# One fused attention and expert kernel: a head's bucket bits from four 32-column tiles, and new orders of TensorE and of the copies

## The chip, the cores and the metric

The kernel runs on one core of one Trainium2 chip. The metric is device time in microseconds (us). Beside it there is one profiled execution, whose trace names every instruction with its start and duration. Engines are named as in the profile: PE is TensorE's matrix multiply, PEld its weight load, DVE VectorE, ACT ScalarE, POOL GpSimd, SP the engine that issues nearly all transfers. TensorE's granted clock is 1.00 of its upper level (2.4 GHz) in every stretch of the execution before.

## The reference, cut to what matters

Sixteen heads (2 batches of 8) of 768 tokens and 64 features. Six projections give each query and key six sign bits; a query sees only the keys with the same six bits.

```
q_bits = (einsum('bhsd,dk->bhsk', q, proj) > 0)          # proj is 64 x 6
k_bits = (einsum('bhsd,dk->bhsk', k, proj) > 0)
mask   = q_bucket[..., :, None] == k_bucket[..., None, :]  # bucket = sum of bits * 2**j
scores = where(mask, scale * q @ k.T, -1e9)
attn   = softmax(scores)
x      = (attn @ v) as 1536 tokens x 512 features
x      = max(x @ w1, x @ w2, x @ w3) @ w_out             # 768 hidden features
out    = g(x @ w_in) @ w_out2                            # 2048 hidden features, g piecewise
```

## The kernel before, in words

Attention fills roughly the first 207 us, the two expert layers the rest. The first expert matmuls stand behind the last attention matmul on PE.

Of attention the work is cut into 96 tiles of 128 queries against all 768 keys, six tiles to a head. A tile goes through: the score block `t_qk` on PE (four matmuls into one of two `s_ps` buffers; the mask is part of the matmul, since rows 64 to 75 of `qb` and `hi` hold scaled bits); `t_max` on DVE; `t_exp` on ACT; then either six transposes `t_tr` on PE into `t_ps` and a copy `t_out` on ACT or DVE (head 0 and the odd heads), or `t_turn` on DVE ("turned" heads: 2, 4, and so on to 14). Three transposed tiles make a group, and `g_pv` multiplies it by the values on PE into `u_ps` in two pieces: first 2 matmuls, then 4. A turned head is multiplied by `block4`: 96 matmuls on tiles of 32 rows by 64 columns that run side by side. `g_copy` and `copy4` on ACT empty the results, and SP folds and moves them.

Bits of head h are made ahead of its first tile. `bits_both` puts two matmuls of 64 columns and 384 tokens into `pj_ps` (the two halves of the head, one in partitions 0 to 63, one in 64 to 127). Two comparisons `bits_rows` on DVE write 44 rows by 384 tokens each into rows 64 to 107 of `qb`: the query's bits stand where they are used, and the key's bits in rows 96 to 107 are moved by one transfer, `prep_move(h, "kb")`, into rows 64 to 75 of `hi`. Then the head's first score block may start.

The order of everything is made when the program is built. PE's order is written by hand as strings: `q5` is the score block of the tile in slot 5, `t` its transposes, `b` the bits that go with a group, `v` and `w` the first and second piece of a group's (or turned head's) value matmuls, `r` the transposition of row sums, `m` an early piece of the first expert layer. `first_part` stands first, `period` five times, `last_part` last. For the other engines a planner (`Work`) walks through tasks with an assumed cost, an assumed `lag` after it (for a transfer: until it has landed) and a due time shifted by `SHIFT`, and writes instructions in the order in which it would start them. The hardware then runs each engine's list in that order.

Of the kernel before, what the change touches and what calls it, by code (L numbers as in the profile page):

```python
# [22 lines left out]
HALF = S // 2  # L23
MASKED = 1.0e9
# [89 lines left out]
def lsh_attention_moe_kernel(  # L114
# [29 lines left out]
    pj_raw = const.tile([128, 64], F32, name="pj_raw")  # L144
# [137 lines left out]
    def attention(mlp_steps):  # L282
        with ExitStack() as ax, ExitStack() as sx:
# [54 lines left out]
            def pj_sign():  # L338
                rows = pj_raw.rearrange("p (a b) -> p a b", a=2)[:, :, 0:6]
                nc.gpsimd.tensor_scalar(out=rows, in0=rows, scalar1=-1.0, scalar2=0.0, op0=ALU.mult, op1=ALU.add)  # L340
# [58 lines left out]
            def bits_mm(h, half, bank, first):  # L399
                nc.tensor.matmul(  # L400
                    out=bank[first:first + 64, 0:HALF], lhsT=pj_raw if h else pj_sc,
# [98 lines left out]
            ahead = s_ps[1][:, 0]  # L500
# [111 lines left out]
            nc.gpsimd.tensor_tensor(out=pj_sc, in0=pj_raw, in1=pj_by, op=ALU.mult)  # L612
# [20 lines left out]
            T_AT, P_AT = 2, 1  # L633
            START = {h: min(SLOT[NK * h + t] for t in range(NK)) for h in range(NH)}
# [4 lines left out]
            SHIFT = {t_exp: 42.5, t_out: 2.0, g_copy: 17.5, copy4: -82.0, pair_copy: -20.5, w_tick: 60.0, bits_rows: 4.5, t_max: -12.5, t_turn: 8.0, pair_recip: 20.0}  # L639
# [8 lines left out]
            scaled, moves, r_place, order = {}, {}, {}, {}  # L648
            raw_s["prep"].free.pop()
            raw_s["r"].free.pop()  # L650

            def head_tasks(h):
# [14 lines left out]
                q = task("SP", 0.6, due, prep_both, h, after=[hi], lag=4)  # L667
                ql = task("SP", 0.5, due + 1, prep_move, h, "ql", after=lo, lag=3.5)
                kh = task("SP", 0.5, due + 2, prep_move, h, "kh", after=[ql], lag=3.5)
                scaled[h], moves[h], r_place[h] = hi, [q, ql, kh], rp  # L670
                if h == 1:
                    bp = place("b", 1)
                    mm = task("PE", 0.644, due + 1, bits_both, h, after=[hi], takes=[bp], leaves=[rp])
                    order["bits"] = [mm]
                    rows = [
                        task("DVE", 0.69, due + 1, bits_rows, h, half, pj_ps, 64 * half, after=[mm]) for half in range(2)
                    ]
                    rows[1]["leaves"] = [bp]
                    bits_task(h, rows, due + 1)
# [431 lines left out]
```

## Time and profile before

| what | before |
|---|---|
| median of 3 runs | 668.01 us (667.34 to 668.87) |
| the profiled execution's own time | 667.27 us |
| its span in the profile | 665.5 us |
| PE busy over the span | 658.9 us (99%) |
| DVE, ACT, POOL busy | 488.2, 340.6, 275.5 us |
| last attention matmul to first expert block on PE | at 207.3 us |

The span is what the profile's instructions cover; the execution's own time holds 1.77 us more. PE's busy time counts a matmul from its start to the end of its own pipeline, so that neighbours overlap: what a block costs is read from its start to the start of the next block.

### The profile page before, as it was taken

To read this page: it belongs to the slowest core of one execution; us is meant where nothing else is said; L and a number is where in the kernel's file an instruction comes from. 1 tells how busy PE (TensorE), PEld (TensorE's weight loads), DVE (VectorE), ACT (ScalarE), POOL (GpSimd) and SP (SyncE) were. 2 spreads that over 40 slices of the span, in tenths; PEclk is the share of its full clock that TensorE was granted. 3 is DMA by queue.
4 is the path that set the end of the run, shared out by engine and by line. 5 is a ranking of instruction groups with operands and counts; after the bars stand their busy time and mean duration, and the time that the engine had idled before them with its cause. 6 is when DMAs were issued, how large, how long until landed. Compare 5 with 4: busy or idle time off the path is not lost.

```text
span 665.5 us, 11771 instructions
## 1 busy us (share of the span) xinstructions
PE 658.9 (99%) x4541; PEld 528.6 (79%) x4541; DVE 488.2 (73%) x718; ACT 340.6 (51%) x631; POOL 275.5 (41%) x252
## 2 busy tenths in 40 slices
PE   8999999999999999999999999999999999999998
PEld 6668777767767888888888888888888888888886
DVE  6788889999764667875443456766888888888844
ACT  7687787887782233232222326665444444444430
POOL 6526647766323335343222113634444444444430
PEclk9999999999999999999999999999999999999999
DMA  7857687785243122321111122121111111211104
GB/s 199 218 123 199 186 222 195 184 246 149 83 124 82 65 95 89 101 86 50 47 49 56 63 65 93 38 80 44 63 64 65 63 65 63 64 63 64 33 0 189
DMA packets 27855, 66.99 MB, mean 101 GB/s; under 512 B 4164, under 2 KB 9124, under 8 KB 27800
## 3 DMA queue, kind: packets, MB, share of 16 engines
q1 hardware_dynamic: 27488, 66.21, 34.0%
q8 instruction: 35, 0.57, 0.4%
q14 instruction: 20, 0.16, 0.1%
q10 hardware_dynamic: 312, 0.04, 0.0%
HBM read 46.17 MB, written 3.19 MB: 74 GB/s over the span
## 4 chain that ended last, share of the span: by engine, by line
PE 97%; DVE 1%; issue 1%; ACT 1%; DVEq 0%; ACTq 0%
PE b L271 49%; PE b L1026 20%; PE s_ps L424 6%; PE t_ps L457 6%; PE u_ps L518 5%; PE s_ps L427 5%; PE u_ps L485 3%; PE pj_ps L400 2%; PE t_ps L485 1%; PE t_ps L307 0%; DVE p L434 0%; ACT pt L467 0%; PE pj_ps L485 0%; PE s_ps L271 0%; DVE pt L467 0%
## 5 line engine op out<-in xcount | busy, mean ns | idle before, releaser
L271 PE MATMUL b<-x_hl,wx 128*128 128x512 f32 x684 | 159.6, 389 | 0.0
L271 PEld LDWEIGHTS b<-x_hl,wx 128*128 128x128 f32 x684 | 128.4, 188 | 26.6
L271 PE MATMUL b<-x_hl,w 128*128 128x512 f32 (+1 forms) x564 | 123.8, 376 | 0.0
L271 PEld LDWEIGHTS b<-x_hl,w 128*128 128x128 f32 x564 | 100.9, 188 | 19.8 <-issue 0.6
L926 POOL TENSOR_TENSOR g<-r,g 128x512 fp32r<-128x512 f32 x48 | 62.5, 1304 | 121.4 <-ACT g L925 121.4
L434 DVE TENSOR_SCALAR_CACHE_REDUCE p<-s_ps 128x768 f32<-128x768 f32 x96 | 89.8, 951 | 11.8 <-PE s_ps L427 8.0
L207 DVE SCALAR_TENSOR_TENSOR wg<-wg,wr 128x512 f32<-128x512 f32 (+1 forms) x58 | 67.9, 1170 | 37.7 <-ACT wg L205 36.9
L449 ACT ACTIVATE p<-p,nm 128x768 f32<-128x768 f32 x96 | 89.7, 936 | 6.7 <-DVE p L434 6.2
L424 PE MATMUL s_ps<-lo,q 128*128 128x384 f32 x192 | 72.0, 375 | 1.1 <-DVE p L434 0.9
L234 POOL TENSOR_TENSOR wx<-wg,wx 128x512 fp32r<-128x512 f32 (+1 forms) x32 | 45.6, 1426 | 65.4 <-ACT wx L228 48.4
L1026 PE MATMUL b<-wx,g 128*128 128x512 f32 x288 | 72.1, 389 | 0.0
L1026 PE MATMUL b<-w,g 128*128 128x512 f32 (+1 forms) x294 | 71.3, 385 | 0.0
L228 ACT CAST wx<-wg 128x512 fp32r<-128x512 f32 (+1 forms) x32 | 19.4, 606 | 92.6 <-DVE wg L220 92.6
L1006 DVE SCALAR_TENSOR_TENSOR r<-r,b 128x512 f32<-128x512 f32 x48 | 33.0, 687 | 44.3 <-ACT r L1005 44.3
L427 PE MATMUL s_ps<-hi,q 76*128 76x384 f32 x192 | 65.4, 340 | 0.0
L1026 PEld LDWEIGHTS b<-w,g 128*128 128x128 f32 x294 | 54.5, 188 | 11.1
L1026 PEld LDWEIGHTS b<-wx,g 128*128 128x128 f32 x288 | 54.1, 188 | 11.2
L1033 DVE TENSOR_TENSOR acc<-b,acc 128x512 f32<-128x512 f32 (+1 forms) x85 | 56.3, 676 | 7.7 <-PE b L1026 7.6
L212 DVE TENSOR_SCALAR wg<-wg 128x512 int32<-128x512 int32 (+1 forms) x58 | 54.2, 935 | 2.7
L234 POOL TENSOR_TENSOR w<-wg,w 128x512 fp32r<-128x512 f32 (+1 forms) x26 | 35.9, 1381 | 47.6 <-ACT w L228 37.4
L1004 ACT ACTIVATE r<-b,half_sb 128x512 f32<-128x512 f32 x48 | 33.0, 688 | 41.2 <-PE b L271 41.2
L228 ACT CAST w<-wg 128x512 fp32r<-128x512 f32 (+1 forms) x26 | 15.9, 610 | 74.5 <-DVE wg L220 74.4
(97 smaller groups left out, 1070.2 us busy)
## 6 DMA issues: line engine op xcount, KB each, us to landing
wr<-in_w SPq DMA_DIRECT2D x48, 512.0 KB
r<-in_kq SPq DMA_DIRECT2D x15, 384.0 KB
q<-hi SPq DMA_DIRECT2D x15, 384.0 KB
v<-in_v SPq DMA_DIRECT2D x21, 256.0 KB
rb<-d SPq DMA_DIRECT2D x16, 192.0 KB
wr<-in_w SPq DMA_DIRECT2D x8, 384.0 KB
q<-lo SPq DMA_DIRECT2D x15, 192.0 KB
lo<-hi SPq DMA_DIRECT2D x15, 192.0 KB
```

The source lines that it names most:

```text
L207: nc.vector.scalar_tensor_tensor(out=f32(g), in0=f32(g), scalar=TINY_SQ, in1=f32(high), op0=ALU.is_ge, op1=ALU.mult)
L212: nc.vector.tensor_scalar(out=g2, in0=g, scalar1=3, scalar2=0x3FFFFFF8, op0=ALU.logical_shift_left, op1=ALU.bitwise_and)
L234: nc.gpsimd.tensor_tensor(out=w[:, 1, 0:cols], in0=f32(g2), in1=f32(w[:, 0, 0:cols]), op=ALU.subtract)
L271: nc.tensor.matmul(out=outp, lhsT=w_[a], rhs=x_[b_], start=(begins and i == 0 and jj == 0), stop=(ends and i == n - 1 and jj == 2),)
L424: nc.tensor.matmul(out=o, lhsT=hd["qa"][:, qs], rhs=hd["lo"][:, ks], start=True, stop=False)
L427: nc.tensor.matmul(out=o, lhsT=hd["qb"][0:76, qs], rhs=hd["hi"][0:76, ks], start=False, stop=True)
L434: nc.vector.tensor_scalar(out=p.rearrange("p (a k) -> p a k", a=2), in0=s_ps[bank.at][:, :, 0:HALF], scalar1=MASKED, scalar2=MASKED, op0=A ...
L449: nc.scalar.activation(out=p, in_=p, func=ACTF.Exp, scale=-1.0, bias=tl[n]["nm"], accum_out=sums_of(h // 2)[:, c:c + 1],)
L457: nc.tensor.transpose(out=t_ps[:, half, j * 128:(j + 1) * 128], in_=tl[n]["p"][:, kt * 128:(kt + 1) * 128], identity=ident,)
L926: nc.gpsimd.tensor_tensor(out=dst[:, 1, cs], in0=src, in1=f32(dst[:, 0, cs]), op=ALU.subtract)
L1026: nc.tensor.matmul(out=pb[:, cs], lhsT=gs[f][:, a, tsl], rhs=wt[:, b_, cs], start=(n == 0), stop=(n == len(terms) - 1),)
L1033: nc.vector.tensor_tensor(out=acc[:, t, cs], in0=pb[:, cs], in1=acc[:, t, cs], op=ALU.add)
```

## The change

It does four things. The bits of heads 1 to 15 come from four matmuls of 32 columns and 192 tokens, one to each quarter of the head, each into its own 32 partitions of `pj_ps` (head 0 stays as it was). Two comparisons of 56 rows by 192 tokens cover two quarters each, and since the second quarter's rows then stand in other partitions, three transfers of 12 rows by 2 x 192 tokens bring the bits into place instead of one of 12 rows by 768. The bits' matmuls need only the scaled head (`prep_scale`), not its rounded copy. PE's order strings are new, and the planner has new costs, lags (4.2 or 5 us for most head transfers, 3 to 4 before) and shifts. The early expert piece sits in `s_ps[0]` in place of `s_ps[1]`. `pj` has 96 columns in place of 64.

```diff
-            def bits_both(h):
-                for half in range(2):
-                    bits_mm(h, half, pj_ps, 64 * half)
+            def bits_four(h):
+                for c in range(4):
+                    nc.tensor.matmul(
+                        out=pj_ps[32 * c:32 * c + 32, 0:QUART], lhsT=pj_raw[:, 64:96],
+                        rhs=head[h]["r"][:, c * QUART:(c + 1) * QUART], start=True, stop=True,
+                    )
+
+            def bits_two(h, half):
+                rows = slice(64 * half, 64 * half + 56)
+                nc.vector.tensor_scalar(
+                    out=head[h]["qb"][64:120, half * HALF:half * HALF + QUART], in0=pj_ps[rows, 0:QUART],
+                    scalar1=pc_sb[rows, 2:3], scalar2=pc_sb[rows, 3:4], op0=ALU.is_gt, op1=ALU.mult,
+                )
+
+            def bits_move(h, to, at, odd):
+                def side(t, rows, o):
+                    return f32(t[rows]).rearrange("p (a b k) -> p a b k", a=2, b=2)[:, :, o]
+
+                hd = head[h]
+                nc.sync.dma_start(out=side(hd[to], slice(64, 76), odd), in_=side(hd["qb"], slice(at, at + 12), 0))
...
-            ahead = s_ps[1][:, 0]
+            ahead = s_ps[0][:, 0]
...
-            SHIFT = {t_exp: 42.5, t_out: 2.0, g_copy: 17.5, copy4: -82.0, pair_copy: -20.5, w_tick: 60.0, bits_rows: 4.5, t_max: -12.5, t_turn: 8.0, pair_recip: 20.0}
+            SHIFT = {prep_scale_act: -13.0, prep_hi: -44.0, t_exp: 37.5, t_out: -23.0, g_copy: 4.0, copy4: 4.0, pair_copy: -101.5, w_tick: 38.0, bits_two: 3.5, t_max: -40.5, t_turn: 12.0, pair_recip: 25.5}
...
-                ready[h] = [task("SP", 0.8, due, prep_move, h, "kb", after=rows + [q], lag=2.5), q, ql, kh]
+            def bits_tasks(h, due, due_rows, due_move, bp):
+                mm = task("PE", 0.48, due, bits_four, h, after=[scaled[h]], takes=[bp], leaves=[r_place[h]])
+                rows = [task("DVE", 0.42, due_rows, bits_two, h, half, after=[mm, placed[h]]) for half in range(2)]
...
+                ready[h] = [
+                    task("SP", 0.5, due_move + 0.1 * j, bits_move, h, *x, after=rows + [q, placed[h]], lag=4.2)
+                    for j, x in enumerate((("hi", 76, 0), ("qb", 96, 1), ("hi", 108, 1)))
+                ] + [q, ql, kh]
...
-                "q22 q24 v19 w19 t21 q25 q26 v20 w20 q27 t23 q30 q28 t25 b25 q29 q35 t27 v25 w25 q31 r25 "
-                "t29 q32 b31 q33 t31 "
+                "q22 q24 r13 v19 t21 w19 q26 q25 v20 w20 q27 t23 q30 b25 q28 t25 q29 q31 t27 v25 w25 t29 "
+                "q32 q33 b31 q35 t31 "
...
-    for rows, c0 in ((slice(0, 64), 32), (slice(64, 128), 0)):
+    for rows, c0 in ((slice(0, 64), 32), (slice(64, 128), 0), (slice(0, 64), 76), (slice(64, 128), 64)):
```

What this moves is seen at three places. The first is PE's list at the first bits of head 1. Before, behind the second score block (the `s_ps_122` rows are its end):

```order
L424 MATMUL s_ps_122<-lo,q 128x384
L427 MATMUL s_ps_122<-hi,q 128x384
L400 MATMUL pj_ps<-r,pj_raw 64x384 x2
L424 MATMUL s_ps_121<-lo,q 128x384
L427 MATMUL s_ps_121<-hi,q 128x384
```

And now, behind the third score block and the first transposes:

```order
L441 MATMUL s_ps_121<-lo,q 128x384
L444 MATMUL s_ps_121<-hi,q 128x384
L474 MATMUL t_ps<-ident,p 128x128 x6
L415 MATMUL pj_ps<-r,pj_raw 32x192 x4
L474 MATMUL t_ps<-ident,p 128x128 x6
```

Two matmuls have become four smaller ones, and they stand one score block and one set of transposes later.

The second place is PE's list at the first group of the repeating part, where its value matmuls (`u_ps<-pt,vr`, in `v19` and `w19`) meet the transposes of slot 21. Before:

```order
L518 MATMUL u_ps<-pt,vr 64x384 x6
L457 MATMUL t_ps<-ident,p 128x128 x6
L424 MATMUL s_ps_121<-lo,q 128x384
L427 MATMUL s_ps_121<-hi,q 128x384
L424 MATMUL s_ps_121<-lo,q 128x384
```

Now:

```order
L582 MATMUL pj_ps<-ident,sums 12x128
L535 MATMUL u_ps<-pt,vr 64x384 x2
L474 MATMUL t_ps<-ident,p 128x128 x6
L535 MATMUL u_ps<-pt,vr 64x384 x4
L441 MATMUL s_ps_122<-lo,q 128x384
```

The transposes have moved in between the two pieces, and the row-sum transposition (`ident,sums`) stands ahead of the first. Before, one group in the whole program was split so; now eight are.

The third place is SP's list at head 1: before, the key's bits (`hi<-q 12x768`) went in one transfer.

```order
L336 DMA v_241<-in_v 128x512
L385 DMA hi<-q 12x768
L395 DMA q<-hi 64x2x768
L385 DMA lo<-hi 64x768
L385 DMA q<-lo 64x768
```

Now:

```order
L337 DMA v_241<-in_v 128x512
L432 DMA hi<-q 12x2x192
L432 DMA q<-q 12x2x192
L432 DMA hi<-q 12x2x192
L386 DMA lo<-hi 64x768
L396 DMA q<-hi 64x2x768
```

Three transfers stand where one stood, and head 1's last move (`lo<-hi`) comes behind them.

## Rows read from the trace of the kernel before

**Rows 1.** Busy time by stage (stretch; its length; each engine; clock; DMA).

```profile
0.00:35.00 35.00, 32.33 (x307) 22.66 (x307) 24.66 (x51) 25.74 (x52) 20.69 (x32) 1.00 0.77 202
35.00:180.00 145.00, 144.57 (x1865) 108.20 (x1864) 129.18 (x232) 113.28 (x224) 82.33 (x90) 1.00 0.67 178
180.00:207.00 27.00, 26.59 (x326) 19.31 (x325) 16.14 (x29) 18.99 (x40) 8.54 (x9) 1.00 0.37 105
```

**Rows 2.** The chain that ended last, from 200 us (start, us, what).

```profile
207.29 212.94 PE b L271 x972
```

**Rows 3.** Waits of the weight loads and of PE's first matmul (us, times, longest).

```profile
PEld s_ps L424 <- DVE p L434: 8.8, 16, 1.2
PEld s_ps L427 <- DMA hi<-q: 0.2, 1, 0.2
PE t_ps L307 <- DVE half_sb L1060: 1.1, 1, 1.1
```

**Rows 4.** PE in order of time, 61 to 70 us (start, duration, line, tiles).

```profile
61.09 0.82 PE L457 MATMUL t_ps<-ident,p 128*128 128x128 f32 x6
61.66 0.42 PE L424 MATMUL s_ps<-lo,q 128*128 128x384 f32 x1
...
62.46 0.38 PE L424 MATMUL s_ps<-lo,q 128*128 128x384 f32 x1
...
63.21 0.82 PE L457 MATMUL t_ps<-ident,p 128*128 128x128 f32 x6
63.96 0.87 PE L400 MATMUL pj_ps<-r,pj_raw 128*64 128x384 f32 x4
64.75 0.44 PE L424 MATMUL s_ps<-lo,q 128*128 128x384 f32 x1
...
65.58 0.34 PE L424 MATMUL s_ps<-lo,q 128*128 128x384 f32 x1
...
66.28 0.82 PE L457 MATMUL t_ps<-ident,p 128*128 128x128 f32 x6
67.03 2.16 PE L518 MATMUL u_ps<-pt,vr 128*64 128x384 f32 x12
69.12 0.44 PE L424 MATMUL s_ps<-lo,q 128*128 128x384 f32 x1
```

**Rows 5.** PE in order of time, 19.2 to 23 us.

```profile
19.30 0.87 PE L457 MATMUL t_ps<-ident,p 128*128 128x128 f32 x6
19.93 0.42 PE L424 MATMUL s_ps<-lo,q 128*128 128x384 f32 x1
...
20.72 0.34 PE L424 MATMUL s_ps<-lo,q 128*128 128x384 f32 x1
...
21.51 0.87 PE L400 MATMUL pj_ps<-r,pj_raw 128*64 128x384 f32 x4
```

**Rows 6.** PE in order of time, 33 to 42 us: the one split group.

```profile
37.43 1.51 PE L518 MATMUL u_ps<-pt,vr 128*64 128x384 f32 x8
38.87 0.44 PE L424 MATMUL s_ps<-lo,q 128*128 128x384 f32 x1
```

**Rows 7.** PE in order of time, 4 to 5 us: head 0's bits, two passes.

```profile
4.04 0.54 PE L400 MATMUL pj_ps<-r,pj_sc 128*64 128x384 f32 x1
...
4.41 0.49 PE L400 MATMUL pj_ps<-r,pj_sc 128*64 128x384 f32 x1
```

**Rows 8.** PE in order of time, 59.6 to 59.9 us: two steps of `block4`.

```profile
59.68 0.32 PE L485 MATMUL u_ps<-dt,v 32*64 32x192 f32 x1
...
59.84 0.32 PE L485 MATMUL u_ps<-dt,v 32*64 32x192 f32 x1
```

**Rows 9.** DVE in order of time, 88 to 91 us: head 8's comparisons.

```profile
88.37 1.37 DVE L407 TENSOR_SCALAR q<-pj_ps,pc_sb 44x384 fp32r<-44x384 f32 x2 [0.48 <-ACT p L449]
```

**Rows 10.** SP's issues in order of time, 89 to 98 us: head 8's bits.

```profile
92.54 0.80 SPq L385 DMA_DIRECT2D hi<-q  x1
```

**Rows 11.** PE in order of time, 96.5 to 98.2 us: head 8's first score block.

```profile
97.12 0.42 PE L424 MATMUL s_ps<-lo,q 128*128 128x384 f32 x1
```

More of the change, by code (lines that the diff above doesn't have):

```diff
@@ L23 @@
 HALF = S // 2
+QUART = S // 4
 MASKED = 1.0e9
@@ L716, in tile_tasks @@
                 takes = own(sums_p, "sums", h // 2, 1)
-                qk = task("PE", 0.72, m, t_qk, n, sp, after=ready[h], takes=[sp], leaves=[h_place[h]])
-                mx = task("DVE", 1.04, m, t_max, n, sp, after=[qk], takes=[pp], leaves=[sp])
-                ex = task("ACT", 1.13, m, t_exp, n, after=[mx], takes=takes, lag=0.1)
+                qk = task("PE", 0.712, m, t_qk, n, sp, after=ready[h], takes=[sp], leaves=[h_place[h]])
+                mx = task("DVE", 0.9, m, t_max, n, sp, after=[qk], takes=[pp], leaves=[sp], lag=0.13)
+                ex = task("ACT", 0.97, m, t_exp, n, after=[mx], takes=takes, lag=0.05)
                 exps[n] = ex
@@ L723, in tile_tasks @@
                     pt_p_[n] = place("dt", 1)
[L724 removed]
+                    tu = task("DVE", 0.9, m - 1, t_turn, n, after=[ex] + outs.get(h, [])[-1:], takes=[pt_p_[n]], leaves=[pp], lag=0.1)
                     outs.setdefault(h, []).append(tu)
@@ L732, in tile_tasks @@
                 for half in range(2):
-                    tr = task("PE", 0.288, m - 4, t_tr, n, half, after=[ex, tr], takes=[] if half else [tb], leaves=[pp], lag=0.1)
+                    tr = task("PE", 0.327, m - 4, t_tr, n, half, after=[ex, tr], takes=[] if half else [tb], leaves=[pp], lag=0.1)
                     order[f"tr{n}"] = order.get(f"tr{n}", []) + [tr]
@@ L737, in tile_tasks @@
                     hs = slice(half, half + 1) if alone else slice(0, 2)
-                    ways = [("ACT", 0.48 if alone else 0.76, nc.scalar.copy), ("DVE", 0.556 if alone else 0.955, nc.vector.tensor_copy)]
+                    ways = [("ACT", 0.48 if alone else 0.7, nc.scalar.copy), ("DVE", 0.556 if alone else 0.955, nc.vector.tensor_copy)]
                     if alone and half:
                         ways.reverse()
-                    cp = task(*ways[0][:2], m - 4, t_out, n, hs, ways[0][2], after=[tr], takes=[pt_p_[g]] if r == 0 and (half == 0 or not alone) else [], leaves=[tb])
+                    cp = task(*ways[0][:2], m - 4, t_out, n, hs, ways[0][2], after=[tr], takes=[pt_p_[g]] if r == 0 and (half == 0 or not alone) else [], leaves=[tb], lag=0.1)
                     if alone:
@@ L751, in group_tasks @@
                 if bits:
-                    bm = task("PE", 0.644, m + 0.4, bits_both, bits, after=[scaled[bits]], takes=[bp], leaves=[r_place[bits]])
-                    order[f"bits{g}"] = [bm]
-                    rows = [task("DVE", 0.69, m - 3, bits_rows, bits, half, pj_ps, 64 * half, after=[bm]) for half in range(2)]
-                    rows[1]["leaves"] = [bp]
-                    rows[1]["after"].append(rows[0])
-                    bits_task(bits, rows, START[bits] - 6)
+                    order[f"bits{g}"] = [bits_tasks(bits, m + 0.4, m - 3, START[bits] - 6, bp)]
                 last = None
@@ L1088 @@
     for rows, first, top in ((0, edge, 1.0), (6, past, 1.0), (32, past, BIG), (38, edge, BIG)):
-        pc[rows:rows + 6] = pc[rows + 64:rows + 70] = [first, top, -0.5 if first > 0 else 0.5, 0.5 * top]
+        pc[rows:rows + 6, 0:2] = pc[rows + 64:rows + 70, 0:2] = [first, top]
+        for at in range(rows % 32 + (12 if top > 1 else 0), 128, 32):
+            pc[at:at + 6, 2:4] = [first, top]
     mw = {n: np.asarray(a) for n, a in inputs.items() if n.startswith("moe")}
```

58 lines of the change are left out of this document (26 added, 32 removed).

## The prediction, made before the changed kernel had run

> **What bounds the kernel now.** I read the stages first [rows 1]. From 35 to 180 us PE is busy for 144.57 of 145.00 us, DVE for 129.18, ACT for 113.28, and the clock is 1.00 throughout. In the first 35 us PE is idle for 2.67 us, of which 1.1 is the wait for the very first operand [rows 3], and from 180 to 207 us for 0.41. So attention is a queue of PE work with about 2.4 us of idle time that something else could cause or end (2.67 + 0.43 + 0.41 - 1.1). Then the chain [rows 2]: from 207.29 us PE multiplies expert blocks without a break for 212.94 us. The change touches nothing behind that point, so what attention gains or loses, the end gains or loses.
>
> Since a matmul's busy time overlaps its neighbour's, a block's price is the distance between starts [rows 4]. A score block q costs 0.70 between a q and a t (65.58 to 66.28), 0.80 after t (61.66 to 62.46), 0.83 after bits (64.75 to 65.58) and 0.79 before bits (20.72 to 21.51) [rows 5]. Transposes t cost 0.57 before q (61.09 to 61.66), but 0.75 before bits (63.21 to 63.96) and 0.75 before value matmuls (66.28 to 67.03), and 0.63 after value matmuls (19.30 to 19.93) [rows 5]. So what costs is passing between blocks that use the whole array (q, t, r) and blocks that use parts of it (b, v, w): 0.18 where t stands before them, 0.09 where q does, and 0.06 for t behind them.
>
> **The change, part by part: the bits.** They cost 0.79 now, from 63.96 to 64.75 [rows 4]. Head 0's, which the trace shows apart, run as two passes: the second starts 0.37 after the first (4.04 to 4.41) [rows 7], with both 64-column tiles going side by side. A pass over 384 tokens shows 0.32 where `block4`, with 192 tokens a pass, steps on every 0.16 us (59.68 to 59.84) with eight tile passes in a step [rows 8]. Four tiles of 32 columns pass over 192 tokens, so if all four go side by side each of the two passes is 0.16 shorter: 0.79 - 0.32 = 0.47. No row shows four column tiles at once. Bounds: one step of 0.16 if nothing but that is left, and 0.79 if only two tiles go at a time (two steps in each pass). I take 0.47, since the rows nearest to it, those of `block4`, keep eight tiles going. Fifteen heads times 0.32 is -4.8 us (bounds -9.5 and 0).
>
> The Trainium skill, "TensorEngine Tiling (Array Packing)", section "Available Configurations", lists 128 by 32 as four independent tiles. By it the sum would be the same -4.8.
>
> **PE's new order.** I expanded both lists of strings and counted neighbours. Transposes directly before b, v or w: 17 before, 16 now, -0.18. Score blocks before b, v or w: 16 and 16, nothing. Row sums r before v: none before, 7 now; no row shows that pair, so I take q's 0.09 (bounds 0 and t's 0.18): +0.63. Transposes behind b, v or w: 10 before, 17 now, 7 x 0.06 = +0.42. Groups whose two pieces are split: 1 before, 8 now. Unsplit they cost 2.09 together (67.03 to 69.12) [rows 4]; apart, w alone costs 1.44 (37.43 to 38.87) [rows 6], and v alone has the form of today's bits, two matmuls of 64 columns, so 0.79: 2.23, that is +0.14 each and +0.98 for seven. Score blocks behind such blocks are one fewer, and one more follows t: about -0.1. Together +1.7 us (bounds +1.1 and +2.4 by r's). This speaks against the change: the order gives back a third of what the bits save.
>
> The same page's section "Key Properties" says that a change of tiling mode drains TensorE; the 0.18, 0.09 and 0.06 above are what that costs in this trace. It gives no price, and the sum goes by the rows.
>
> **Comparisons.** Two of 1.37 together [rows 9] become two of 56 by 192. The element count of a row halves; at best half of 1.37 goes, at worst nothing: 0 to 0.69 a head, up to 10 us of DVE over 15 heads. DVE is not the bound (129.18 of 145), so I book 0 for it; PE's own queue covers it. If that cover were gone it would be a gain.
>
> **Moves.** One issue of 0.80 [rows 10] becomes three, with 1.6 us more on SP for each head and 24 us in all. Queued behind them on SP are the next head's load, its other moves and the folds; who waits in the end is a head's first score block. For head 8, the tightest that I found, the comparisons end at 89.74, the transfer is issued from 92.54 to 93.34, and its first q starts at 97.12 [rows 9 to 11]: 3.8 us for landing, without a wait for it; the one wait of PE for such a transfer in the whole trace is 0.2 [rows 3]. In the new order even heads have 10.3 us from bits to first q by the prices above, against 9.74 by the same prices before (+0.56); the bits end 0.32 earlier, the comparisons perhaps 0.3, and the third issue ends 1.6 later. That leaves 3.8 + 0.56 + 0.32 + 0.3 - 1.6 = 3.4 us. It is closer by 0.4, and the third transfer carries half the bytes (18 KB against 36 KB). I take 0, with bounds of 0 and 0.6 for each of seven even heads (0.4 plus the 0.2 seen): +4.2.
>
> **Start and end.** Of the bits' 4.8 us three heads' worth (0.96) falls into the first 25 us, where the waits of [rows 1] lie and PE waits for softmax rather than for itself. In the new list the first bits no longer fill the time between the second and third score block. On the other side there is less for DVE to do, which PE waits for longest (8.8 us at the weight loads, mostly hidden behind running matmuls) [rows 3]. At the end, `w91` now stands directly before the last `block4`, which needs `u_ps` emptied first, and the transposes and expert piece that covered this copy are elsewhere. These pull both ways; I take the idle time as unchanged, with bounds of -2.4 (all of it gone) and +2.4 (doubled). The larger `pj` (48 KB against 32 KB) arrives at the start; a part of a microsecond there is covered by DVE, which makes head 0's `lo` before it compares. I book 0. Making the bits after the scaling alone, and the early expert piece in the other buffer, cost PE nothing.
>
> **Sum.** -4.8 + 1.7 = -3.1 us. Against the profiled execution's 667.27 (span 665.5 and 1.77 around it) that is 664.2. That execution lies 0.74 below the median of the runs, 668.01, and set against the median the forecast is 664.9 us.
>
> **The rivals.** *Two tiles at a time.* If four column tiles on one row group do not run together, bits stay at 0.79 and only the order's +1.7 is left: 669.7, slower. For it: only two column tiles are seen side by side here [rows 7], and all four would stream through all 128 rows, while `block4`'s use 32 each. Against it: eight tiles in a step [rows 8]. It decides from 0.68 us a block on, where 15 blocks save less than 1.7 us. Chance 0.09.
>
> *The third move comes late.* PE then waits at a head's first q, in the place of the shorter bits. It decides from 0.44 us at each of the seven even heads (3.1 / 7); with 0.6 at each it is -3.1 + 4.2 = +1.1 (669.1), and with 1.3 at each +6.0 (674). For it: SP's issue time grows, and 3.4 us is less than any margin now. Against it: half the bytes, and bits that come earlier. Chance 0.10. The Trainium skill, "DMA: Bandwidth & Descriptors", section "Rules for kernel authors", speaks for this rival: transfers under 64 KB are mostly overhead and should be put together. By it three moves of 18 KB cost nearly three times one of 36 KB; no run yet shows how much of that lies on the path.
>
> *The waits eat it.* The three early heads' 0.96 are lost to the start, the copy before the last `block4` shows, and some waits on DVE and ACT come in the place of the time saved: 1.0 to 2.4 us back, 665.9 to 667.3, of which most lies within 0.2% of before. Chance 0.16.
>
> *More than that.* The new orders also end the waits of today, down to -3.1 - 2.4: 662.5 us. Chance 0.18.
>
> **How the numbers follow.** The forecast (663.7 to 665.9) has 0.47. A measurement of this kernel can hardly tell less than 0.2% (1.34 us) from no change. Faster by more than that: the forecast, the last rival and about a third of the third, 0.47 + 0.18 + 0.05 = 0.70. Slower by more: the first rival, and half of the second, 0.09 + 0.05 = 0.14. Within 0.2%: 0.16. The likeliest sign holds most of the chance. The range reaches from 662.0, a little below the case where all waits go, to 668.8, where the moves are late enough to cancel the gain: what lies outside is about 0.05 below and 0.14 above.
>
> **What would show it.** On PE, bits 0.47 from their start to the next block's, and two passes about 0.21 apart; if 0.79, the first rival. Transposes between v and w at 0.81, v alone at 0.79, w at 1.44. The first expert block at about 204.2 us in place of 207.29, and everything behind it shifted by that. On SP three issues of about 0.8 for each head; at the weight loads, waits for `hi` or `q` transfers at `t_qk` of a few tenths at most. The prediction is wrong if bits cost more than 0.68, if those waits add up to more than 2 us, or if PE's idle time in the first 35 us grows by more than 1 us.

## The result, and the profile after

The changed kernel takes 671.84 us (median of 9 runs, 670.00 to 675.89), the kernel before 667.74 (9 runs, 666.74 to 668.87): ratio 1.0058, 95% interval 1.0036 to 1.0081, slower by 2.4 to 5.4 us. The forecast was 664.9. The profiled execution took 675.89 us, the longest of the nine, so sizes read from its trace are on the high side.

The chain first (the instructions that released one another up to the last one). The time is lost ahead of the first expert block, as the prediction had it, which now starts at 215.94 us in place of 207.29 [rows 2], with transfers on the way. Start, duration, what, in us:

```profile
31.49 3.98 DMA vr<-in_v
...
95.12 2.73 DMA hi<-q
...
119.19 3.90 DMA hi<-q
...
146.91 2.12 DMA hi<-q
...
215.94 212.94 PE b L272 x972
```

By stage (columns as in [rows 1]), the time is not lost where PE was known to be idle:

```profile
0.00:35.00 35.00, 32.05 (x315) 22.29 (x315) 23.39 (x50) 23.71 (x47) 17.86 (x29) 1.00 0.77 200
35.00:180.00 145.00, 139.52 (x1710) 103.07 (x1710) 122.27 (x223) 109.97 (x219) 79.64 (x87) 0.98 0.68 178
180.00:216.00 36.00, 34.31 (x535) 25.06 (x532) 21.28 (x40) 22.89 (x48) 13.24 (x15) 1.00 0.32 95
```

PE's idle time in the first 35 us is 2.95 against 2.67, but from 35 to 180 us it is 5.48 against 0.43, and from 180 us to the expert blocks 1.69 against 0.41. The clock is 0.98 in the middle stage, where it was 1.00. What PE's matmuls wait for between 8 and 207 us (total, times, longest):

```profile
PE s_ps L444 <- DMA hi<-q: 4.0, 3, 2.6
PE t_ps L474 <- DVE pt L484: 1.4, 3, 0.7
PE s_ps L441 <- DVE p L451: 0.8, 2, 0.5
PE t_ps L474 <- ACT pt L484: 0.7, 1, 0.7
PE u_ps L502 <- issue: 0.7, 1, 0.7
PE u_ps L502 <- ACT uo L552: 0.6, 1, 0.6
```

At the weight loads before there was one wait for such a transfer, of 0.2 [rows 3]. Now matmuls wait 4.0 us for three.

The bits themselves came out as forecast. PE in order of time, then VectorE's two comparisons of the same head:

```profile
62.93 0.34 PE L444 MATMUL s_ps<-hi,q 76*128 76x384 f32 x1
63.20 0.53 PE L415 MATMUL pj_ps<-r,pj_raw 128*32 128x192 f32 x8
63.66 0.44 PE L441 MATMUL s_ps<-lo,q 128*128 128x384 f32 x1
```

```profile
64.31 0.47 DVE L422 TENSOR_SCALAR q<-pj_ps,pc_sb 56x192 fp32r<-56x192 f32 x1
...
65.81 0.49 DVE L422 TENSOR_SCALAR q<-pj_ps,pc_sb 56x192 fp32r<-56x192 f32 x1
```

The block costs 0.46 (63.20 to 63.66), as against 0.79 [rows 4]: four column tiles do run side by side. A comparison takes 0.48, as against 0.68.

The longest of the three waits is at head 12. PE, then SyncE's list ahead of it:

```profile
145.61 0.82 PE L474 MATMUL t_ps<-ident,p 128*128 128x128 f32 x6
146.19 0.42 PE L441 MATMUL s_ps<-lo,q 128*128 128x384 f32 x1
149.17 0.66 PE L444 MATMUL s_ps<-hi,q 76*128 76x384 f32 x1 [2.56 <-DMA hi<-q]
```

```profile
134.51 0.60 SPq L386 DMA_DIRECT2D q<-lo  x1
...
137.97 0.54 SPq L325 DMA_DIRECT2D r<-in_kq  x1
142.72 0.46 SPq L386 DMA_DIRECT2D lo<-hi  x1
143.23 0.58 SPq L337 DMA_DIRECT2D v<-in_v  x1
143.90 0.86 SPq L432 DMA_DIRECT2D hi<-q  x1
144.81 0.83 SPq L432 DMA_DIRECT2D q<-q  x1
145.69 0.54 SPq L562 DMA_DIRECT2D uc<-uo  x1
146.33 0.54 SPq L563 DMA_DIRECT2D u<-uo  x1
146.91 0.85 SPq L432 DMA_DIRECT2D hi<-q  x1
```

The comparisons of head 12 end at 138.93, but SyncE stands from 138.51 to 142.72 at `lo<-hi`, which may not overwrite `lo` until `q<-lo`, issued at 134.51, has landed. The three moves come behind it, the third behind two folds as well, and PE has already started on the head. After the wait the clock is down (columns as in [rows 1], the last three are clock, DMA share, GB/s):

```profile
146.00:150.00 4.00, 1.44 (x8) 1.21 (x7) 1.53 (x4) 2.36 (x5) 2.20 (x3) 0.85 0.50 124
150.00:155.00 5.00, 5.00 (x19) 2.95 (x19) 3.80 (x6) 1.24 (x4) 3.76 (x4) 0.50 0.94 268
```

From 150 to 155 us PE is busy at 0.50, the lower of its two levels (1.2 GHz). By the two levels about half of those 5 us (an estimate) is lost on top of the wait of 2.6.

To see all of it, I compared each block's distance to the next block's start with the prices that the prediction read from [rows 4 to 6]. By them PE's work fell by 3.4 us (3.1 forecast); the first score block starts 0.7 later (7.57 against 6.83); and the waits are 17.7 us where they were 6.4. Such a split takes the prediction's prices over, but those that can be read anew hold: bits 0.46 for 0.47, v alone 0.80 for 0.79, w 1.44, transposes between the two 0.80 for 0.81, and row sums 0.20 before v where they take 0.11 before transposes, the 0.09 of the sum. So the forecast sum of PE's work held, and waits of 11 us came on top in this execution.

### The profile page after: what moved, and what is told of

Read it like the earlier page. It is cut to its first block, busy times and chain, and to the rows that moved or that the text cites. A ratio compares the mean times of both kernels' runs of the same rounds, so it can differ in the third digit from the quotient of the medians.

```text
span 674.1 us, 11961 instructions
## 1 busy us (share of the span) xinstructions
PE 660.9 (98%) x4601; PEld 528.6 (78%) x4601; DVE 484.8 (72%) x721; ACT 339.0 (50%) x628; POOL 274.7 (41%) x252
## 4 chain that ended last, share of the span: by engine, by line
PE 91%; DMA 3%; DVE 2%; ACT 1%; SPq 1%; issue 1%; POOL 0%; DVEq 0%; ACTq 0%; POOLq 0%
PE b L272 48%; PE b L1039 19%; PE u_ps L535 5%; PE t_ps L474 5%; PE s_ps L441 4%; PE s_ps L444 4%; PE u_ps L502 3%; DMA hi<-q 1%; ACT p L466 1%; PE t_ps L502 1%; DVE p L451 1%; DMA uc<-u 1%; PE pj_ps L415 1%; DMA vr<-in_v 1%; DVE pt L484 0%
## 5 line engine op out<-in xcount | busy, mean ns | idle before, releaser
L1039 PEld LDWEIGHTS b<-w,g 128*128 128x128 f32 x294 | 54.5, 188 | 11.1
```

The costliest lines, as they stand in the source:

```text
L1039: nc.tensor.matmul(out=pb[:, cs], lhsT=gs[f][:, a, tsl], rhs=wt[:, b_, cs], start=(n == 0), stop=(n == len(terms) - 1),)
```

## The experiments

Ratios are to runs of the kernel before on the same chip.

| kernel | what it is | us, median (runs) | ratio, 95% interval |
|---|---|---|---|
| again | the changed kernel once more | 672.97 (6) | 1.0069, 1.0048 to 1.0089 |
| orders_only | its orders, old bits, one move | 675.21 (6) | 1.0091, 1.0067 to 1.0115 |
| bits_only | its bits, planned anew in the old PE order | 679.11 (4) | 1.0152, 1.0130 to 1.0173 |
| moves_first | its moves issued as early as they can be | 670.55 (12) | 1.0047, 1.0026 to 1.0067 |
| old_ends | the same, with the old first and last strings | 671.19 (7) | 1.0051, 1.0033 to 1.0068 |
| four_cmp_new | four comparisons and one move, in its orders | 683.23 (5) | 1.0229, 1.0208 to 1.0251 |
| four_cmp_old | the same, planned anew in the old PE order | 672.67 (6) | 1.0073, 1.0051 to 1.0094 |
| extra_issues | before, two unread transfers a head, planned | 674.97 (6) | 1.0107, 1.0077 to 1.0137 |
| extra_in_place | before, the same two, nothing else moved | 669.44 (11) | 1.0028, 1.0007 to 1.0049 |
| bits_in_place | new bits and three moves, all orders as before | 671.44 (10) | 1.0062, 1.0040 to 1.0085 |
| four_in_place | four matmuls and comparisons, one move, orders as before | 669.59 (11) | 1.0029, 1.0015 to 1.0043 |
| bits_alone | four matmuls, the rest as before | 667.37 (12) | 0.9991, 0.9975 to 1.0006 |
| moves_pool | bits_in_place, two of three moves on GpSimd | 667.40 (12) | 0.9989, 0.9971 to 1.0007 |
| pool_padded | that, 20 more TensorE instructions at the start | 667.02 (12) | 0.9989, 0.9969 to 1.0010 |
| after_pool | the changed kernel, two of three moves on GpSimd | 672.08 (12) | 1.0057, 1.0038 to 1.0077 |
| new_plan | before with the planner's new numbers only | 675.77 (5) | 1.0112, 1.0088 to 1.0136 |
| strings_only | before with PE's new strings only | 678.86 (4) | 1.0166, 1.0152 to 1.0179 |
| shift_one | before with one planner shift changed | 671.29 (6) | 1.0062, 1.0044 to 1.0080 |

**again.** No edit.

> The changed kernel a second time, for a second trace of it. Theory A (the head's bits arrive late because three moves stand on SP behind a move that waits for another transfer): 670 to 673 us, bits 0.46 us, and waits at the second matmul of a head's first score block in some heads, but not the same size in each execution. Theory B (the new order of TensorE and of the copies itself makes PE wait, at the start, at the end and for DVE): the same time, but waits that repeat in the same places.

The loss is the same, its place is not: here head 8's first score block waits 2.5 us for the move and head 12's does not. Which head is hit differs between the two executions.

**orders_only** gives the changed kernel the old bits back, **bits_only** gives the old kernel the new bits. orders_only, against the changed kernel:

```diff
-                mm = task("PE", 0.48, due, bits_four, h, after=[scaled[h]], takes=[bp], leaves=[r_place[h]])
+                mm = task("PE", 0.796, due, bits_both, h, after=[scaled[h]], takes=[bp], leaves=[r_place[h]])
...
-                    task("SP", 0.5, due_move + 0.1 * j, bits_move, h, *x, after=rows + [q, placed[h]], lag=4.2)
...
+                ready[h] = [task("SP", 0.8, due_move, prep_move, h, "kb", after=rows + [q, placed[h]], lag=4.2), q, ql, kh]
```

and bits_only, against before:

```diff
-                    bm = task("PE", 0.644, m + 0.4, bits_both, bits, after=[scaled[bits]], takes=[bp], leaves=[r_place[bits]])
+                    bm = task("PE", 0.48, m + 0.4, bits_four, bits, after=[scaled[bits]], takes=[bp], leaves=[r_place[bits]])
...
-                ready[h] = [task("SP", 0.8, due, prep_move, h, "kb", after=rows + [q], lag=2.5), q, ql, kh]
...
+                    task("SP", 0.8, due + 0.1 * j, bits_move, h, *x, after=rows + [q], lag=2.5)
```

> The changed kernel with the old bits (two matmuls of 64 columns, two comparisons of 44 x 384, one move of 12 x 768) in the new order of TensorE, and the new planner. PE work is 1.7 us more than before by the prices of neighbours. Theory A: SP has 30 issues fewer, so the late moves go and it stands 1 to 3 us above before, 669 to 671 us. Theory B: the waits stay and PE work is 4.9 us more than in the changed kernel, 674 to 677 us.

> The kernel before with the bits part alone: four 32-column matmuls, two short comparisons and three moves; TensorE's order and the planner's other costs, lags and shifts as before. PE work is 15 x 0.33 = 4.9 us less. Theory A: part of it is lost at the heads' first score blocks, 664 to 668 us, with waits for hi or q moves. Theory B: nothing is lost but a little at the start, 662.5 to 664 us.

The new orders alone lose 6.1 us (4.5 to 7.7), where their price was put at +1.7. On top of them the new bits, with their moves, give back about 2 (1.0058 against 1.0091), not 4.8. And the new bits alone lose 10 us when the planner writes the other engines' lists anew around them, though PE's strings are the old ones. Neither half is good by itself.

The 6.1 us are not all the orders' doing, as the trace shows. In the profiled execution of orders_only the small matmuls on zeros ahead of the first score block step on every 0.11 us, in that of before every 0.06:

```profile
8.75 0.30 PE L315 MATMUL t_ps<-warm 32*64 32x32 f32 x2
8.86 0.29 PE L315 MATMUL t_ps<-warm 32*64 32x32 f32 x2
9.10 0.69 PE L448 MATMUL s_ps<-lo,q 128*128 128x384 f32 x1
```

```profile
6.60 0.22 PE L314 MATMUL t_ps<-warm 32*64 32x32 f32 x2
6.66 0.23 PE L314 MATMUL t_ps<-warm 32*64 32x32 f32 x2
6.83 0.44 PE L424 MATMUL s_ps<-lo,q 128*128 128x384 f32 x1
```

PE steps at about half its pace up to 13.4 us, though the granted clock reads 1.00 there. The first score block starts 2.3 us late, and the first three take 4.56 us (3.35 in the changed kernel's trace): about 3.5 of the 8.7 us that this execution loses ahead of the expert blocks. Another 2.2 stand inside `block4` (below), 1.7 are the forecast price of the orders, and 1.3 are left for all other waits. new_plan's trace (further down) has the same slow start, the 18 others don't: their first score blocks start at 6.80 to 8.22. Whether the other executions of these two kernels start slowly too is not shown.

**moves_first** and **old_ends** ask whether the late moves and the ends carry it. moves_first, against the changed kernel:

```diff
-                    task("SP", 0.5, due_move + 0.1 * j, bits_move, h, *x, after=rows + [q, placed[h]], lag=4.2)
+                    task("SP", 0.5, due_move - 30 + 0.1 * j, bits_move, h, *x, after=rows + [q, placed[h]], lag=4.2)
```

old_ends is moves_first with the strings `first_part` and `last_part` of before (the row sums that `period` now issues left out there).

> The changed kernel with one number changed: the three moves are due 30 slots earlier, so that the planner writes them ahead of whatever else SP has ready. PE's order is the same. Theory A: the waits at the first score blocks go, 666 to 669 us. Theory B: 670 to 672 us as the changed kernel, since PE's order has not moved.

> The kernel with the moves first, with the first part and the last part of PE's order as before (the row sums of two pairs moved to where the new period has them). If the waits of the first 25 us and of the last 10 us come from the new strings: 667 to 669 us, 2 to 3 us less than with the moves first (670.6). If not: 670 to 672 us.

In the trace of moves_first the waits of PE for `hi<-q` are gone, yet the ratio falls only from 1.0058 and 1.0069 to 1.0047, that is 0.7 to 1.5 us, and the intervals overlap. By the same account as above its waits still add up to 14 us: a value load that is late at `v8` (1.3), pauses inside `block4` (4.3, as against 1.5 before; see below), transposes that wait for copies. The end strings make no difference.

**four_cmp_old, four_cmp_new** avoid the added moves with four comparisons of 24 rows by 192 tokens:

```diff
+            def bits_one(h, c):
+                rows = slice(32 * c, 32 * c + 24)
+                nc.vector.tensor_scalar(
+                    out=head[h]["qb"][64:88, c * QUART:(c + 1) * QUART], in0=pj_ps[rows, 0:QUART],
+                    scalar1=pc_sb[rows, 2:3], scalar2=pc_sb[rows, 3:4], op0=ALU.is_gt, op1=ALU.mult,
+                )
```

> The kernel before with the four 32-column matmuls, but four comparisons of 24 x 192 (one to a quarter), each written to where its quarter belongs, so that one move of 12 x 768 is enough as before; all orders as before. PE work is 4.9 us less, SP has the issues of before, DVE has about 0.5 us more a head. Theory A (the three moves are what costs): 663 to 665.5 us. Theory B (shorter bits are eaten by other waits whatever the moves): 667 to 669 us.

> The changed kernel with the same four comparisons and one move, in the new order. Theory A: the late moves go as with moves first, 668 to 670.5 us; what is left above 665 is the new order's waits at the start and the end. Theory B: 671 to 674 us.

Neither gains. The expectation of the first took all orders to stay, but with the new costs the planner writes them anew, so these two do not tell the bits from the plan; four_in_place, below, asks it again with the lists kept. In the new orders the longer comparisons hold `pj_ps`, for which the row sums wait that now stand ahead of the value matmuls. From the weight loads' waits of four_cmp_new:

```profile
PEld pj_ps L579 <- DVE q L422: 10.9, 6, 1.8
```

**extra_issues, extra_in_place** add two unread 12x2x192 transfers behind each head's one move, first as steps of the planner, then with all lists as before. extra_issues:

```diff
+                for o in range(2):
+                    task("SP", 0.8, due + 0.1, bits_extra, h, o, after=[kb])
```

and extra_in_place:

```diff
+            def bits_extra(h):
+                prep_move(h, "kb")
+                for o in range(2):
+                    to, at = [f32(head[h]["qb"][rows]).rearrange("p (a b k) -> p a b k", a=2, b=2)[:, :, o] for rows in (slice(112, 124), slice(96, 108))]
+                    nc.sync.dma_start(out=to, in_=at)
```

> The kernel before with two more transfers of 12 x 2 x 192 behind each head's key move, into rows that nobody reads and nobody waits for. If 30 more issues of 0.8 us on SP and their traffic delay the other transfers: 670 to 676 us, with waits at heads' first score blocks. If only the wait for the third move costs: 667.5 to 669 us.

> The kernel before with all its orders and its bits kept, and two unread 12x2x192 transfers issued right behind each head's one move on SyncE. The kernel with such transfers as planned steps of their own took 674.97 us. If two more issues and their traffic cost that by themselves: 670 to 675 us. If what it paid for was the plan that they changed: 667.0 to 668.5 us.

The same transfers cost 7.2 us planned and 1.9 us in place. So 5 us of the first are the reordering, and what 24 us more of SyncE issue time and the traffic cost by themselves is 0.5 to 3.3.

**bits_in_place, four_in_place.** From here on the lists of before are kept instruction for instruction, apart from the bits; the planner is told the old costs. bits_in_place, against before:

```diff
-                    bm = task("PE", 0.644, m + 0.4, bits_both, bits, after=[scaled[bits]], takes=[bp], leaves=[r_place[bits]])
+                    bm = task("PE", 0.644, m + 0.4, bits_four, bits, after=[scaled[bits]], takes=[bp], leaves=[r_place[bits]])
...
-                ready[h] = [task("SP", 0.8, due, prep_move, h, "kb", after=rows + [q], lag=2.5), q, ql, kh]
+                ready[h] = [task("SP", 0.8, due, bits_moves, h, after=rows + [q], lag=2.5), q, ql, kh]
```

four_in_place has one 12x768 move in place of `bits_moves`, and two of the 24x192 comparisons in each comparison's place.

> The kernel before with its four engine orders kept instruction for instruction; only head 8's and later heads' bits differ: four 128x32 matmuls where two 128x64 stood, each comparison as one 56x192 instruction where 24x384 stood, and the three moves issued one behind the other where the one move stood. Theory A (the two added issues and their traffic cost, wherever they stand): SP is held about 1.6 us longer at each of 15 heads, first score blocks wait for the third move, 666 to 672 us, no gain over before or a loss. Theory B (the cost of the change lies in the newly written orders, not in the bits): the shorter bits give their 15 x 0.32 us = 4.8 us or most of it, 663 to 664.5 us.

> The kernel before with its four engine orders kept; four 128x32 matmuls for the bits, each of the two comparison steps as two 24x192 comparisons (so VectorE is held longer, not shorter), and the one 12x768 move kept. No transfer is added. If the bits' 0.32 us a head reach the end of the kernel when nothing else is moved: 663 to 664.5 us. If shorter bits are eaten by waits elsewhere, or the longer comparisons of VectorE (about 0.2 us a step) are paid by TensorE: 666.5 us or more.

Both lose, so theory B (all of it is reordering) falls too. (The edit of bits_in_place is wider than its expectation says: the bits of heads 1 to 15 change, and comparisons of 44x384 stood there.) bits_in_place has the slower SyncE, four_in_place the slower VectorE (134.6 us busy of the 145 us stage, against 129.2 [rows 1]). What the shorter bits do with neither is the next question.

**bits_alone** has four matmuls, comparisons as long as before and the one move: each comparison reads the 192 tokens of one tile twice, so the bits of the other two quarters are left out. **moves_pool** is bits_in_place with two of three moves issued by GpSimd. bits_alone, against bits_in_place:

```diff
-                    out=head[h]["qb"][64:120, half * HALF:half * HALF + QUART], in0=pj_ps[rows, 0:QUART],
+                    out=out, in0=pj_ps[rows, 0:QUART].unsqueeze(1).to_broadcast([44, 2, QUART]),
```

and moves_pool, against bits_in_place (after_pool: the same line, against the changed kernel):

```diff
-                nc.sync.dma_start(out=side(hd[to], slice(64, 76), odd), in_=side(hd["qb"], slice(at, at + 12), 0))
+                (nc.gpsimd if odd else nc.sync).dma_start(out=side(hd[to], slice(64, 76), odd), in_=side(hd["qb"], slice(at, at + 12), 0))
```

> The kernel before with all its orders kept, the four 128x32 matmuls for the bits of heads 1 to 15, two comparisons of 44 rows by 384 tokens as before (they read the 192 tokens of a tile twice, so half of the bits come from the wrong tokens: the output is not the reference's) and the one 12x768 move. So TensorE's bits are 0.32 us shorter at 15 heads and nothing else is longer or added. Theory A (what was lost in the kernels in place is the price of the added issues and of the longer comparisons): about 4 us faster than before, 663 to 664.5 us. Theory B (TensorE stands in a cycle with VectorE and ScalarE, whose order leaves it nothing to gain): 666.5 to 668 us, with waits at score blocks and transposes that grow by the 4.8 us taken away.

> As the kernel with the bits in place (671.44 us: old orders, four matmuls, two 56x192 comparisons, three moves behind one another), but the second and third move are issued by GpSimd's queue, so that SyncE issues one transfer a head as before. Theory A (the moves cost by SyncE's issue time and by what is queued behind them): 664 to 667 us, at or below before. Theory B (they cost by their landing): 670 to 672 us, with waits of the weight loads for hi and q transfers as before. GpSimd's own issue time, which no row of this kernel shows, could delay its scalings and folds; then waits name GpSimd.

> The changed kernel (671.84 and 672.97 us) with the second and third move of each head issued by GpSimd's queue and nothing else moved. In the old orders this took 4.0 us off (671.44 to 667.40). Theory A (the moves on SyncE are the largest part of what failed): 667.5 to 669.5 us, and no wait of 0.8 us or more at the first score blocks of heads 8, 10 and 12. Theory B (TensorE's new strings and the planner's new orders are): 670 us or more, with the waits elsewhere unchanged.

bits_alone is the plainest test of the prediction's sum: 4.8 us less work on PE, nothing else longer. The time falls by 0.6 us (from 1.7 faster to 0.4 slower). In its profiled execution the expert blocks start 1.0 us earlier than before. Since PE's blocks stand in the same order as before in bits_alone, moves_pool and pool_padded (below), their times from start to start can be set against before's one by one (us, one execution each; `block4` by itself):

| against before | bits_alone | moves_pool | pool_padded |
|---|---|---|---|
| start of the first score block | +0.57 | +0.38 | +0.87 |
| 15 blocks of bits | -4.93 | -4.93 | -4.93 |
| 7 `block4` | +1.47 | +3.82 | +1.33 |
| all other blocks | +1.86 | +0.33 | +0.37 |
| start of the expert blocks | -1.04 | -0.40 | -2.36 |

The bits give what was forecast. In bits_alone half of what is lost again is in blocks that wait for their neighbours; in moves_pool nearly all of it is in `block4`. But extra_in_place, with PE's list of before, has 1.92 more in `block4` as well, so these sums differ between executions without any change on PE. Head 8 shows one of the waits in bits_alone. PE, then SyncE:

```profile
95.31 0.82 PE L468 MATMUL t_ps<-ident,p 128*128 128x128 f32 x6
95.88 0.42 PE L435 MATMUL s_ps<-lo,q 128*128 128x384 f32 x1
96.83 0.45 PE L438 MATMUL s_ps<-hi,q 76*128 76x384 f32 x1 [0.54 <-DMA hi<-q]
```

```profile
92.63 0.54 SPq L557 DMA_DIRECT2D u<-uo  x1
93.22 0.80 SPq L386 DMA_DIRECT2D hi<-q  x1
```

PE reaches the head at 95.88, where it was 97.12 [rows 11]; the move is issued at 93.22, where it was 92.54 [rows 10], since SyncE stands before a `lo<-hi` ahead of it for 3.1 us (0.7 before) until a `q<-lo` has landed. A faster PE does not bring that landing forward: PE has caught up with the move, and waits 0.54.

moves_pool against bits_in_place (0.9989 and 1.0062) is worth about 4.9 us: in the old orders what the three moves cost is that SyncE issues two more a head. The Trainium skill, "DMA: Bandwidth & Descriptors", section "Rules for kernel authors", says that spreading transfers over issuing engines gives no bandwidth and only saves issue time. Here moving the two issues to GpSimd was worth those 4.9 us. In the changed kernel the same edit does nothing (1.0057 against 1.0058): head 8 still waits 1.7 us for a `hi<-q`, which SyncE and GpSimd there issue within 1 us of each other. So, to within the 2 us or so of the two intervals, SyncE's issue time is not what holds the changed kernel back.

**new_plan, strings_only, shift_one** take the orders apart, with the bits of before. strings_only has the changed kernel's `first_part`, `period` and `last_part` (the diff ahead of the prediction shows a part of them) and lets the planner write the other lists by its old numbers. new_plan has the new costs, lags, due times and `SHIFT` with PE's strings as before; the early expert piece's buffer and the bits made after the scaling alone are the changed kernel's too. shift_one, against before:

```diff
-            SHIFT = {t_exp: 42.5, t_out: 2.0, g_copy: 17.5, copy4: -82.0, pair_copy: -20.5, w_tick: 60.0, bits_rows: 4.5, t_max: -12.5, t_turn: 8.0, pair_recip: 20.0}
+            SHIFT = {t_exp: 42.5, t_out: -2.0, g_copy: 17.5, copy4: -82.0, pair_copy: -20.5, w_tick: 60.0, bits_rows: 4.5, t_max: -12.5, t_turn: 8.0, pair_recip: 20.0}
```

> TensorE's order and the bits of the kernel before, one move a head, and only the planner's new lags, due times and shifts, which reorder ScalarE, VectorE, GpSimd and SyncE. The kernel with the new TensorE order too, and the old bits, took 675.21 us. If the orders of the other four engines carry that loss: 671 to 675 us. If TensorE's new order does (1.7 us by its neighbours' prices, and waits at its start and end): 667 to 669.5 us.

> The kernel before with TensorE's new order strings and nothing else: old bits, one move, old planner costs, lags and shifts (the other engines' orders follow by the planner). By neighbours' prices TensorE's work is 1.7 us more. If the strings carry the loss that the new orders with the old bits showed (675.21 us): 673 to 677 us. If the planner's new numbers do (675.77 us alone): 668.5 to 670.5 us.

> The kernel before with one number of the planner changed: the due time of t_out shifted by -2.0 in place of 2.0. TensorE's order stays, ScalarE's, VectorE's and SyncE's lists change at a few places. If the orders of before are a narrow optimum: 669 to 673 us. If small reorderings are free: 667 to 668.5 us.

The strings lose 11.1 us without the numbers, the numbers 7.5 without the strings, together 6.1: they are made for each other, and still lose. (The traces of the second and third have the slow start described above.) In strings_only five row sums wait 1.0 us each for VectorE's bits to leave `pj_ps`; one of them:

```profile
78.52 0.33 PE L427 MATMUL s_ps<-hi,q 76*128 76x384 f32 x1
79.88 0.27 PE L565 MATMUL pj_ps<-ident,sums 128*12 128x128 f32 x1 [1.02 <-DVE q L407]
```

That is the pair "r before v" that the prediction booked at 0.09, for PE's change of tiles. One planner shift, which moves a few copies and transfers, loses 4.1 us (2.9 to 5.3), and the trace shows nearly all of it at one place: head 2's bits now wait 2.08 us for GpSimd's `hi`, and behind that wait the granted clock is 0.50 from 17.5 to 20.9 us: the bits take 1.55, where they took 0.87.

```profile
15.53 0.34 PE L427 MATMUL s_ps<-hi,q 76*128 76x384 f32 x1
17.95 1.55 PE L400 MATMUL pj_ps<-r,pj_raw 128*64 128x384 f32 x4 [2.08 <-POOL hi L368]
```

**pool_padded** follows a pause in moves_pool for which no releaser is named, in the middle of `block4`:

```profile
152.22 0.32 PE L506 MATMUL u_ps<-dt,v 32*64 32x192 f32 x1
154.25 0.38 PE L506 MATMUL t_ps<-dt,v 32*64 32x192 f32 x2 [1.71 <-issue]
```

The DMA view of 151.2 to 151.4 us has an instruction transfer of 16 KB starting there (packets, MB, share):

```profile
q8 instruction: 1, 0.02, 43.7%
```

Such packets come once in about 256 TensorE instructions, and `block4` runs 384 in 4 us. The edit adds 20 instructions ahead of all blocks:

```diff
-                for _ in range(rounds):
-                    for q in range(4):
+                for n in range(4 * rounds + 5):
+                    for q in (n % 4,):
```

> The kernel with the bits in place and two of three moves on GpSimd (667.40 us), with five more of the small 32x32 matmuls that TensorE runs on zeros at the start (about 0.15 us, 20 instructions with their weight loads). Every later instruction of TensorE then stands 20 places further from its 16 KB instruction fetches. If the pauses inside block4 (1.6 and 2.1 us at two heads, 4.2 us in all seven, against 0.4 in the profiled execution before) come from where those fetches fall: the two large ones shrink to 0.5 us or less and the time is 664 to 666 us. If they come from other work (transfers, the copies that empty the buffers): they stay where they are, 667 to 668 us.

What PE's matmuls wait for between 8 and 207 us, in moves_pool and then in pool_padded:

```profile
PE t_ps L506 <- issue: 3.3, 3, 1.7
```

```profile
PE t_ps L506 <- issue: 0.6, 1, 0.6
...
PE pj_ps L506 <- issue: 0.4, 1, 0.4
```

From its first to its last matmul, the block at 149 us goes from 6.07 to 3.83 us (the shortest there is), the one at 102 us from 5.59 to 5.01, and the one at 172 to 174 us from 3.83 to 4.56: in these two traces the place moves with the instruction count. The expectation wanted both large pauses at 0.5 us or less and 664 to 666 us; only one of them went, and the median stays (0.9989 both times). So that the pauses cost the time is not shown, and nothing that ran is shown to beat the kernel before.

## Why the prediction was wrong, step by step

**What bounds the kernel.** "Attention is a queue of PE work", so that what PE saves reaches the end, with the idle time left "as unchanged": this is the step that failed first, and bits_alone shows that it failed, with 0.6 of 4.8 us at the end. PE is busy for 144.57 of 145 us [rows 1], but that does not mean that it is the only bound. The 2.4 us that "something else could cause or end" were too little as well: by the distances between blocks 6.4 us of waits were there before, most of them inside busy time. Where the saving goes is shown for single executions only: in part to blocks that wait for their neighbours, in part to pauses of `block4` (1.5 us before, 2.0 to 6.2 in the 19 other traces), for which the prediction had no term. A busy share does not tell what PE gains by less work.

**Bits**: right, 0.46 for 0.47; the first rival (two tiles at a time) is refuted. **Comparisons**: 0.96 a head for 1.37, booked at nothing. **PE's prices**: right in the sum, -3.4 for -3.1 in the profiled execution, and one by one where they can be read anew.

**PE's new order**, +1.7: the price holds, but a new order also brings waits, and these the prediction set to unchanged. In the changed kernel's trace they grow by 11.3 us: 4.0 at matmuls for the moves, about 3 by the lower clock behind head 12 (an estimate), 0.9 in `block4`, and the rest for copies, comparisons and other transfers. moves_first, whose trace has no wait of a matmul for a move, still stands 3.1 us above before (1.7 to 4.5), where the sum had -3.1. The waits are thus the largest error, and they turn the sign. orders_only's +6.1 is no clean measure of them, for its slow start.

**Moves**, "I take 0, with bounds of 0 and 4.2": mis-sized. In the changed trace the waits for them are 4.0 us at matmuls, and the clock behind head 12 adds about as much as its wait. The slack of 3.4 us at head 8 was worked out from SyncE's issue times and the order's prices. What was left out is what stands ahead of a move in SyncE's list, a wait of 4.2 us for another transfer's landing at head 12. By the trace this is the second rival; moves_first puts its share at 0.7 to 1.5 us of the loss, which the intervals don't tell from nothing. In the old orders the price of three issues is about 4.9 us.

The rule by which the Trainium skill spoke for that rival ("DMA: Bandwidth & Descriptors", "Rules for kernel authors": small transfers are mostly overhead) agrees with the issues: 0.86, 0.83 and 0.85 where one took 0.80 [rows 10].

**Start and end**, "idle time as unchanged": the first 35 us nearly so (2.95 against 2.67); behind 180 us 1.3 us more; the 5 us are in the middle, for which no change was booked at all. Of its three signs of failure, the one on waits for `hi` and `q` transfers was met (4.0, over 2), the other two were not.

**What stays open.** How the 6.1 us of the new orders divide, since strings and numbers lose more apart than together, and how much of them is the slow start of 9.10 against 6.83, which the changed kernel's two traces do not show (7.57 and 6.96). How much of a median `block4`'s pauses cost. And why the added issues on SyncE cost nothing that after_pool could win back.

## What to carry to other kernels

A saving on the busiest engine need not reach the end, even at a busy share of 99.7%: try the saving alone with every list kept, and follow block by block where it goes, before pricing a change. Where the lists of all engines have been fitted to each other, planning them anew can cost more (one shift of a planner: 4.1 us) than the saving brings. Price a move by the list of the queue that issues it, with the waits for landings that stand ahead, not by its own issue and landing. And test the parts of a change in place, with nothing reordered: that separated 1.9 us of transfers from 7.2 us of "transfers and a new plan".

## What the runs showed of the hardware

**A dense block often pauses where an instruction transfer falls.** Over the 20 profiled executions of this study there are 140 `block4`s. 55 have an instruction transfer of queue q8 that starts 0.53 to 1.87 us behind their first matmul (a range picked afterwards, as the one that separates best): all 55 run over 0.1 us longer than the shortest (3.83 us from first to last matmul), by up to 1.75. Of the other 85, 22 do, among them the longest of all, 2.7 us, with the transfer 3.1 us behind the start. This is read off, and moved once by pool_padded; what sets the size is not shown: before and extra_in_place have the same PE list, and their seven blocks are 1.5 and 3.5 us above the shortest.

**The clock falls after a wait and takes its time to come back**: a wait of 2.6 us in the changed kernel, then a granted clock of 0.50 from 150 to 155 us and 0.94 from 155 to 160.

**A comparison's time is not in its rows.** 24 rows by 192 tokens take 475 ns (four_in_place), 56 by 192 478, and 44 by 384 679: 24 and 56 rows take the same, and half the tokens save 0.2 us, not half.
